# Middle rows of a folded Fourier transform: broadcast into both mirror slots and halved in the tables, in place of a zero fill followed by a second transfer

## The chip, the cores and the metric

The kernel runs on one core of one Trainium2 chip. The metric is the device time of one execution in microseconds (us). Each kernel has several executions; the detailed trace of one of them was kept, and that one is called the profiled execution.

## The reference

The input x is 8 batches of 3008 rows of 256 numbers. It is Fourier transformed along the rows and then along the columns, and the real part is fed to a feed-forward block with a squared ReLU.

```python
X = np.fft.fft(x, axis=1)          # x: (8, 3008, 256)
X = np.fft.fft(X, axis=2)
t = X.real.reshape(24064, 256)
h = np.maximum(t @ w_in, 0.0)      # w_in: (256, 2048)
return h * h @ w_out               # w_out: (2048, 256)
```

Inputs and output are float32.

## The kernel before

The row transform is folded by symmetry: rows n, S-n, M-n and M+n (S = 3008, M = 1504) are brought together, so that a quarter of the table is enough. The rows of a batch lie in one tile `x4` with four slots: slots 0 and 1 hold rows going up and are loaded directly by SyncE. Slots 2 and 3 hold their mirror images and are fetched by GpSimd with an indirect gather in reversed order. Each of the first 126 partitions holds six consecutive rows of a slot. Four middle rows (n = 0, 752, 1504 and 2256) have fewer partners than the others, and the kernel before puts a copy of them on an extra partition, 126. That partition is first filled with zeros, for batch 0 by a DMA from a zero tile, and the middle rows are then put over the zeros by two more DMAs, which must wait for the zero fill.

```python
x4 = xp.tile([P, 4, NQ, D], F32, name="x4")
zt = const.tile([2 * NQ, 2 * D], F32, name="zt")
nc.vector.memset(zt, 0.0)
...
xm = x4[NP : NP + 1].rearrange("p s q d -> p (s q) d")

def load_mid(b, eng):
    eng.dma_start(out=xm[:, 1 : NQ + 2 : NQ], in_=x[b : b + 1, 0 : M + 1 : M])
    eng.dma_start(out=xm[:, 3 : 3 * NQ + 3 : 3 * NQ - 1], in_=x[b : b + 1, QN : S : M])
...
nc.scalar.dma_start(out=x4[NP : NP + 1]..., in_=zt)      # zero fill of partition 126
for s in range(2):
    gather(0, 1 - s)                                     # GpSimd: slot 3, then slot 2
    nc.sync.dma_start(out=x4[0:NP, s, :, :], in_=up(0, s))   # SyncE: slot 0, then slot 1
```

The head of the program then runs: VectorE and ScalarE build sine and cosine tables in two halves (`red`, `trig`), GpSimd builds the column matrix and then issues the weights, TensorE runs dummy matmuls on the zeroed tile `ez` ahead of the real work, meant to bring its clock up (in this kernel's trace they start 0.43 us apart at first and 0.21 us apart from 16.07 us on, and the full clock is on record from 16.03 us), and VectorE folds batch 0 (`u`, then `v`, then `w`).

```python
pv.memset(csD[:, 0, 0, P - 1 : P], 1.0)                  # GpSimd
pv.memset(ez, 0.0)
...
for c in range(4):                                       # GpSimd's queue
    nc.gpsimd.dma_start(out=wst[:, :, cs], in_=moe_w_in[:, cs]...)
nc.gpsimd.dma_start(out=wot, in_=moe_w_out...)
for h in range(2):
    for f in rd0[5 * h : 5 * h + 5] + (tr0[3:] if h else tr0[:3]):
        f()
    if h == 0:
        load_mid(0, nc.scalar)
        alt_vecs()
dmats_fin()
sgn_vecs()
for f in mi0 + fe[0:3] + rd1[0:2]:                       # fe: the folds of batch 0
    f()
dmats_hi()
for _ in range(18):
    mm(warm, ez[:, 0, 0, :], ez[:, 0, 0:4, :], True, True)
for f in fe[3:]:
    f()
gcast(0, nc.scalar.copy)                                 # waits for the first weights
gmat(0)
for _ in range(4):
    mm(warm, ez[:, 1, 0, :], ez[:, 1, 0:4, :], True, True)
```

The first fold pair reads slots 0 and 3, and the second reads slots 1 and 2. Both read all 127 partitions, so both need the middle rows. After the fold come the matmuls of the row transform (`pf`), and from then on the main stream (`xb`, `po`).

Of the kernel before, what the change touches and what calls it, by code (L numbers as in the profile page):

```python
# [9 lines left out]
F32 = mybir.dt.float32  # L10
F16 = mybir.dt.float16
I32 = mybir.dt.int32
AF = mybir.ActivationFunctionType
ALU = mybir.AluOpType
# [8 lines left out]
def kernel(  # L23
# [7 lines left out]
    nc = tc.nc  # L31
    B, S, D = x.shape
    _, F = moe_w_in.shape
    P = 128
    M = S // 2
    QN = M // 2
    NQ = 6
    NP = QN // NQ + 1
# [14 lines left out]
    const = ctx.enter_context(tc.tile_pool(name="const", bufs=1))  # L53
# [15 lines left out]
    ts = nc.vector.tensor_scalar  # L69
    stt = nc.vector.scalar_tensor_tensor  # L70
    act = nc.scalar.activation

    def mm(o, l, r, start, stop):
        nc.tensor.matmul(o, l, r, start=start, stop=stop, skip_group_check=True)  # L74

    def iota(name, shape, pattern, base, mult, dt=F32):
        t = const.tile(shape, dt, name=name)
        nc.gpsimd.iota(t, pattern=pattern, base=base, channel_multiplier=mult,
                       allow_small_or_imprecise_dtypes=True)
        return t  # L80

    idx = iota("idx", [P, 1], [[0, 1]], NP - 1, -1, I32)
    pidx = iota("pidx", [P, 1], [[0, 1]], 0, 1)
    nvec = iota("nvec", [P, NQ], [[1, NQ]], 1, NQ)
# [3 lines left out]
                   allow_small_or_imprecise_dtypes=True)  # L88

    x4 = xp.tile([P, 4, NQ, D], F32, name="x4")  # L90
    zt = const.tile([2 * NQ, 2 * D], F32, name="zt")
    ez = const.tile([P, 2, NQ, P], F16, name="ez")
    nc.vector.memset(zt, 0.0)

    def up(b, s):
        return bass.AP(tensor=x.tensor, offset=x.offset + (b * S + s * M + 1) * D,
# [15 lines left out]
    xm = x4[NP : NP + 1].rearrange("p s q d -> p (s q) d")  # L112

    def load_mid(b, eng):
        eng.dma_start(out=xm[:, 1 : NQ + 2 : NQ], in_=x[b : b + 1, 0 : M + 1 : M])
        eng.dma_start(out=xm[:, 3 : 3 * NQ + 3 : 3 * NQ - 1], in_=x[b : b + 1, QN : S : M])

    def load_x(b):
        for s in range(2):
# [1 line left out]
            gather(b, 1 - s)  # L121
        load_mid(b, nc.gpsimd)

    nc.scalar.dma_start(out=x4[NP : NP + 1].rearrange("p s q d -> p (s q d)")
                      .rearrange("p (a c) -> p a c", a=2 * NQ), in_=zt)
    for s in range(2):
        gather(0, 1 - s)
        nc.sync.dma_start(out=x4[0:NP, s, :, :], in_=up(0, s))
# [6 lines left out]
    wS = 2.0 * math.pi / S  # L135
    wD = 2.0 * math.pi / D

    def vec(name, w=1):
        return const.tile([P, w], F32, name=name)

    top = vec("top")
    ts(out=top, in0=pidx, scalar1=float(NP), scalar2=None, op0=ALU.is_equal)
    nval = vec("nval", NQ)
    stt(out=nval, in0=nvec, scalar=QN - 0.5, in1=nvec, op0=ALU.is_lt, op1=ALU.mult)
    stt(out=nval[:, 3:4], in0=top, scalar=float(QN), in1=nval[:, 3:4], op0=ALU.mult, op1=ALU.add)
    hpi = vec("hpi")
    nc.vector.memset(hpi, math.pi / 2)
    hpl = vec("hpl")
    ts(out=hpl, in0=pidx, scalar1=NP - 1.0, scalar2=math.pi / 2, op0=ALU.not_equal, op1=ALU.mult)
    sgn = vec("sgn")  # L150
    s3 = vec("s3")
    nsgn = vec("nsgn")
# [16 lines left out]
    def sgn_vecs():  # L169
        ts(out=sgn, in0=pidx, scalar1=P - 1.5, scalar2=None, op0=ALU.is_lt)  # L170
        ts(out=s3, in0=sgn, scalar1=-2.0, scalar2=None, op0=ALU.mult)
        ts(out=sgn, in0=sgn, scalar1=2.0, scalar2=-1.0, op0=ALU.mult, op1=ALU.add)
        ts(out=nsgn, in0=sgn, scalar1=-1.0, scalar2=None, op0=ALU.mult)

    def absval(o, i):
        ts(out=o.bitcast(I32), in0=i.bitcast(I32), scalar1=0x7FFFFFFF, scalar2=None,
           op0=ALU.bitwise_and)
# [5 lines left out]
    def dmats():  # L183
        pv = nc.gpsimd
        t = tgp.tile([P, P], F32, name="td", tag="td")
        m = tgp.tile([P, P], F32, name="md", tag="md")
        pv.tensor_scalar(out=m, in0=jrow, scalar1=pidx[:, 0:1], scalar2=None, op0=ALU.mult)
        pv.tensor_scalar(out=t, in0=m, scalar1=1.0 / D, scalar2=R23, op0=ALU.mult, op1=ALU.add)
        pv.tensor_scalar(out=t, in0=t, scalar1=R23, scalar2=-float(D),
                         op0=ALU.subtract, op1=ALU.mult)  # L190
        pv.tensor_tensor(m, m, t, op=ALU.add)
        pv.memset(csD[:, 0, 0, P - 1 : P], 1.0)
        pv.memset(ez, 0.0)  # L193

        def fin():
            absval(t, m)
            nc.vector.tensor_copy(csD[:, 0, 1, P - 1 : P], alt)
            act(csD[:, 0, 1, 0 : P - 1], m[:, 0 : P - 1], AF.Sin, bias=0.0, scale=wD)
            act(csD[:, 0, 0, 0 : P - 1], t[:, 0 : P - 1], AF.Sin, bias=hpi[:, 0:1], scale=-wD)

        def hi():
            ts(out=csD[:, 1, :, 0:P:2], in0=csD[:, 0, :, 0:P:2], scalar1=-1.0, scalar2=None,
               op0=ALU.mult)
            nc.vector.tensor_copy(csD[:, 1, :, 1:P:2], csD[:, 0, :, 1:P:2])
        return fin, hi

    cosT = const.tile([P, NQ, HE + HO], F16, name="cosT")
    sinT = const.tile([P, NQ, HE + HO], F16, name="sinT")
    BLK = ((0, HE), (HE, HO))

    def table_ops(blk):
        c0, n = BLK[blk]
        ng = (n + 1) // 2
        nm = n // 2
        cs = slice(c0, c0 + ng)
        tb = {}
        hq = NQ // 2
        kb = krow[:, blk : blk + 1, 0:ng].to_broadcast([P, hq, ng])

        def red(h):  # L220
            qs = slice(h * hq, (h + 1) * hq)

            def views():
                return tb["t"][:, qs, 0:ng], tb["m"][:, qs, 0:ng]

            def nk():
                if h == 0:
                    tb["t"] = tgp.tile([P, NQ, HG], F32, name="tt", tag=f"tt{blk}")
                    tb["m"] = tgp.tile([P, NQ, HG], F32, name="tm", tag=f"tm{blk}")
                vt(views()[1], nval[:, qs].unsqueeze(2).to_broadcast([P, hq, ng]), kb, op=ALU.mult)  # L230

            def near():
                t, m = views()
                ts(out=t, in0=m, scalar1=1.0 / S, scalar2=R23, op0=ALU.mult, op1=ALU.add)

            def turns():
                t, m = views()
                ts(out=t, in0=t, scalar1=R23, scalar2=-float(S), op0=ALU.subtract, op1=ALU.mult)  # L238

            def rest():  # L240
                t, m = views()
                vt(m, m, t, op=ALU.add)  # L242

            def size():
                t, m = views()
                absval(t, m)

            return [nk, near, turns, rest, size]

        def trig(h):  # L250
            qs = slice(h * hq, (h + 1) * hq)

            def cos(qs, bias):
                return lambda: act(cosT[:, qs, cs], tb["t"][:, qs, 0:ng], AF.Sin,
                                   bias=bias[:, 0:1], scale=-wS)

            r = [lambda: act(sinT[:, qs, cs], tb["m"][:, qs, 0:ng], AF.Sin, bias=0.0, scale=wS)]
            if h == 0:
                return r + [cos(slice(0, 1), hpi), cos(slice(1, hq), hpl)]
            return r + [cos(qs, hpl)]  # L260

        src = slice(c0, c0 + nm)
        dst = slice(c0 + n - 1, c0 + n - 1 - nm, -1)

        def mir(d, a, qs, sv):
            o, i = d[:, qs, dst], (d if qs.start % 2 else a)[:, qs, src]
            if blk == 0:
                return lambda: act(o, i, AF.Copy, bias=0.0, scale=sv[:, 0:1])
            return lambda: ts(out=o, in0=i, scalar1=sv[:, 0:1], scalar2=None, op0=ALU.mult)

        qg = (slice(0, 5, 4), slice(2, 3), slice(1, 6, 4), slice(3, 4))
        return (red(0) + red(1), trig(0) + trig(1),
                [mir(cosT, sinT, qs, sv) for qs, sv in zip(qg, (nalt, alt, alt1, nalt))]
                + [mir(sinT, cosT, qs, sv) for qs, sv in zip(qg, (nalt, alt, nalt1, alt))])
# [167 lines left out]
    for g in range(0, NPAIR, CH):  # L442
# [3 lines left out]
        while o < n:  # L446
            b, i = divmod(g + o, NK)
# [90 lines left out]
    rd0, tr0, mi0 = table_ops(0)  # L538
    rd1, tr1, mi1 = table_ops(1)
    dmats_fin, dmats_hi = dmats()  # L540
    for c in range(4):
        cs = slice(c * F // 4, (c + 1) * F // 4)
        nc.gpsimd.dma_start(out=wst[:, :, cs],
                          in_=moe_w_in[:, cs].rearrange("(c p) f -> p c f", p=P))
    nc.gpsimd.dma_start(out=wot, in_=moe_w_out.rearrange("(c p) o -> p c o", p=P))
    for h in range(2):
        for f in rd0[5 * h : 5 * h + 5] + (tr0[3:] if h else tr0[:3]):
            f()
        if h == 0:
            load_mid(0, nc.scalar)  # L550
            alt_vecs()
    dmats_fin()
    sgn_vecs()
    for f in mi0 + fe[0:3] + rd1[0:2]:
        f()
    dmats_hi()
    warm = psx.tile([P, 512], F32, name="warm", tag="x")

    for _ in range(18):
        mm(warm, ez[:, 0, 0, :], ez[:, 0, 0:4, :], True, True)  # L560
    for f in fe[3:]:
        f()
    gcast(0, nc.scalar.copy)
    gmat(0)
    for _ in range(4):
        mm(warm, ez[:, 1, 0, :], ez[:, 1, 0:4, :], True, True)
    gcast(1, nc.scalar.copy)
    gcast(2, nc.vector.tensor_copy)
# [13 lines left out]
    def spread(ops, lo, hi):  # L582
        for i, f in enumerate(ops):
            side.setdefault(lo + int((hi - lo) * i / len(ops)), []).append(f)
# [8 lines left out]
    spread([(lambda c=c: wcast(c)) for c in range(4)], 3, 7)  # L593
    spread(rd1[2:], 1, 8)
    spread(fo, 7, 12)
    spread(tr1[0:3], 6, 8)
    spread(tr1[3:], 8, 9)
    spread(mi1, 9, 12)
    spread(stage1_ops(0, 1, True), 11, 15)
    FOLD = {0: [(1, 0.35, 0.52)], 1: [(2, 0.02, 0.2), (3, 0.38, 0.56), (4, 0.7, 0.85)],  # L600
# [37 lines left out]
    for f in mmq:  # L638
        p = f()
# [32 lines left out]
```

## Time and profile before

| | before |
|---|---|
| time, median of 3 | 659.51 us (659.0 to 660.09) |
| span of the profiled execution (its time was 661.0 us) | 659.22 us |
| landings of x: slots 0, 1, 3, 2 | 6.24, 9.45, 12.15, 14.67 us |
| last middle row landed | 14.66 us |
| first weights: issued, landed | 10.04, 15.75 us |
| first fold pair starts | 14.59 us |
| first `pf` matmul | 21.54 us |
| 19th `pf` matmul (start of the second block) | 45.01 us |
| span minus that | 614.21 us |

The landings and the last rows of this table are read from the trace's DMA and matmul records, counted from the start of the span. At 661.0 us the profiled execution is 1.5 us above the median of the three others, so this trace shows a slower execution than usual.

Two lines of the page's part on the chain that ended last show what bounds the program (share of the span by engine, then by line):

```profile
PE 93%; DVE 4%; DMA 2%; ACT 1%; issue 0%; DVEq 0%
PE po L74 50%; PE xb L74 37%; PE pf L74 6%; DMA x<-zt 1%; DMA x<-in_x_dram 1%; DVE u L314 1%; DVE h L534 0%; DVE h L532 0%; DVE wout L591 0%; DVE v L322 0%; DVE tm L242 0%; DVE tm L230 0%; ACT r L520 0%; DVE w L327 0%; DVE tt L238 0%
```

TensorE (PE) carries 93% of the chain. The change does not touch that stream, so only the other 7%, which lies almost entirely at the start, can move.

The chain in the first 25 us of the kernel before (start in us, length in us, what):

```profile
0.91 0.48 DVE zt L93
1.43 6.74 DMA x<-zt
...
8.19 6.28 DMA x<-in_x_dram
...
14.59 1.82 DVE u L314 x2
...
21.54 3.08 PE pf L74 x18
```

The zero tile, its transfer and the transfer of the middle rows stand one behind the other and end at 14.46 us. The fold follows at once.

The timeline of the same kernel, three instructions of VectorE and two of GpSimd (start, length, engine, line, operation, tiles, and in brackets the engine's idle time just before and what ended it):

```profile
8.46 1.94 DVE L176 TENSOR_SCALAR tt<-tm 128x567 int32<-128x567 int32 x1
14.59 1.82 DVE L314 TENSOR_TENSOR u<-x 127x765 f16<-127x765 f32 x2 [3.38 <-DMA x<-in_x_dram]
21.14 1.16 DVE L327 TENSOR_TENSOR w<-v 127x381 f16<-127x381 f16 x4
```

```profile
8.71 1.37 POOL L193 MEMSET ez<- 128x1536 f16 x1
10.04 3.08 POOL L543 DMA_DIRECT2D wst<-in_moe_w_in_dram  x4
```

VectorE idles for 3.38 us until the middle rows are there. VectorE's absolute-value step took 1.94 us beside GpSimd's memset, where the same step of the first half took 0.46 us.

The view of waits for the first 47 us names the same wait, and a small one for the weights (engine, line, what ended the waiting: us in total, times, longest):

```profile
DVE u L314 <- DMA x<-in_x_dram: 3.4, 1, 3.4
ACT win L282 <- DMA wst<-in_moe_w_in_dram: 0.7, 1, 0.7
```

### The profile page before, as it was taken

What the parts mean: (1) busy time and instruction counts of PE and PEld (TensorE: products, weight loads), DVE (VectorE), ACT (ScalarE), POOL (GpSimd) and SP (SyncE); (2) the same over time, 40 slices, a digit from 0 to 9 for tenths busy, and PEclk for the clock granted to TensorE, in tenths of its full rate; (3) what the DMA queues carried; (4) which work ended last, traced back from release to release, by engine and by line L of the source; (5) the groups of instructions that cost most, each with busy time, mean ns of one, the idle gap of its engine ahead of it and who ended that gap; (6) DMA issues with size and microseconds to landing.
All of it is one profiled execution on the core that took longest, in us unless ns stands there. A gap on an engine that the chain in (4) does not pass through costs nothing.

```text
span 659.2 us, 14938 instructions
## 1 busy us (share of the span) xinstructions
PE 637.7 (97%) x5958; PEld 550.5 (84%) x5958; DVE 404.0 (61%) x1076; ACT 519.0 (79%) x930; POOL 52.2 (8%) x67
## 2 busy tenths in 40 slices
PE   3779999999999999999999999999999999999998
PEld 1358889888798889888898887988899888998886
DVE  7899559679677554865558555455555555444451
ACT  5687777887788888888888887888888888888883
POOL 7203003123020000400000000000000000000000
PEclk9999999999999999999999999999999999999999
DMA  8927217286354111721111101011111111111111
GB/s 265 304 66 186 81 36 213 73 221 157 99 140 133 47 38 44 194 77 49 33 49 33 50 33 49 33 45 39 46 35 49 34 49 41 41 45 45 42 49 50
DMA packets 33756, 54.65 MB, mean 83 GB/s; under 512 B 4438, under 2 KB 28534, under 8 KB 33686
## 3 DMA queue, kind: packets, MB, share of 16 engines
q0 software_dynamic: 6256, 27.45, 15.4%
q1 hardware_dynamic: 27398, 26.22, 12.5%
q8 instruction: 46, 0.75, 0.5%
q14 instruction: 24, 0.20, 0.1%
q10 hardware_dynamic: 32, 0.03, 0.0%
HBM read 29.00 MB, written 24.64 MB: 81 GB/s over the span
## 4 chain that ended last, share of the span: by engine, by line
PE 93%; DVE 4%; DMA 2%; ACT 1%; issue 0%; DVEq 0%
PE po L74 50%; PE xb L74 37%; PE pf L74 6%; DMA x<-zt 1%; DMA x<-in_x_dram 1%; DVE u L314 1%; DVE h L534 0%; DVE h L532 0%; DVE wout L591 0%; DVE v L322 0%; DVE tm L242 0%; DVE tm L230 0%; ACT r L520 0%; DVE w L327 0%; DVE tt L238 0%
## 5 line engine op out<-in xcount | busy, mean ns | idle before, releaser
L74 PE MATMUL po<-wout,h 128*128 128x256 f16 (+1 forms) x3040 | 452.7, 272 | 0.0
L74 PE MATMUL xb<-qt,G 128*128 128x256 f16 (+8 forms) x1760 | 332.2, 257 | 3.3 <-ACT r L520 2.6
L74 PEld LDWEIGHTS <-h 128*128 128x128 f16 (+1 forms) x3040 | 289.9, 97 | 33.6 <-issue 0.2
L534 DVE TENSOR_TENSOR h<-r 128x512 f16<-128x512 f16 (+1 forms) x384 | 160.5, 418 | 239.8 <-ACT r L530 239.1
L520 ACT ACTIVATE r<-xb 128x512 f16<-128x512 f32 (+1 forms) x384 | 226.4, 590 | 98.0 <-PE xb L74 85.8
L74 PEld LDWEIGHTS <-G 128*128 128x128 f16 x2640 | 237.7, 97 | 44.9 <-issue 10.2
L530 ACT ACTIVATE r<-xb 128x512 f16<-128x512 f32 (+1 forms) x384 | 226.2, 589 | 20.4 <-PE xb L74 2.3
L74 PE MATMUL xb<-pt,G 128*128 128x256 f16 (+8 forms) x880 | 187.8, 257 | 0.7 <-ACT G L292 0.3
L532 DVE TENSOR_TENSOR h<-r 128x512 f16<-128x512 f16 (+1 forms) x384 | 158.1, 412 | 0.0
L464 ACT ACTIVATE os<-po 128x512 f32<-128x512 f32 (+1 forms) x95 | 56.3, 592 | 4.0 <-PE po L74 4.0
L74 PE MATMUL pf<-cosT,w 127*128 127x377 f16 (+1 forms) x96 | 28.9, 325 | 2.2 <-DVE w L327 1.8
L314 DVE TENSOR_TENSOR u<-x 127x765 f16<-127x765 f32 x32 | 29.0, 947 | 3.4 <-DMA x<-in_x_dram 3.4
L74 PE MATMUL pf<-sinT,w 127*127 127x377 f16 (+1 forms) x96 | 28.9, 325 | 0.0
L104 POOL DMA_INDIRECT x<-in_x_dram,idx x18 | 26.5, 1471 | 5.4 <-issue 5.1
L74 PEld LDWEIGHTS <-w 127*128 127x128 f16 (+1 forms) x192 | 22.4, 118 | 5.1 <-DVE w L327 2.3
L120 POOL DMA_DIRECT2D x<-in_x_dram x14 | 7.9, 561 | 217.0 <-DVE u L318 217.0
L327 DVE TENSOR_TENSOR w<-v 127x381 f16<-127x381 f16 x64 | 20.4, 352 | 0.0
L369 ACT ACTIVATE as<-pf 128x377 f32<-128x377 f32 (+5 forms) x32 | 15.5, 486 | 3.3 <-PE pf L74 3.0
L74 PEld LDWEIGHTS <-ez 127*128 127x128 f16 (+1 forms) x46 | 5.1, 113 | 15.4 <-POOL ez L193 10.1
L74 PE MATMUL warm<-ez 128*128 128x512 f16 x22 | 8.0, 537 | 10.1 <-POOL ez L193 10.1
L322 DVE TENSOR_TENSOR v<-u 127x768 f16<-127x768 f16 x32 | 16.7, 548 | 0.0
L405 DVE TENSOR_TENSOR pt<-pf,as 128x377 f16<-128x377 f32 (+1 forms) x16 | 8.8, 547 | 0.3
(92 smaller groups left out, 123.6 us busy)
## 6 DMA issues: line engine op xcount, KB each, us to landing
out_dram<-os SPq DMA_DIRECT2D x157, 128.0 KB
x<-in_x_dram POOLq DMA_DIRECT2D x14, 756.0 KB, 10.1
wst<-in_moe_w_in_dram POOLq DMA_DIRECT2D x4, 512.0 KB, 5.7
wot<-in_moe_w_out_dram POOLq DMA_DIRECT2D x1, 2048.0 KB, 13.8
x<-in_x_dram SPq DMA_DIRECT2D x2, 756.0 KB
x<-in_x_dram,idx POOLq DMA_INDIRECT x18, 11.1
x<-in_x_dram POOLq DMA_DIRECT2D x14, 2.0 KB, 10.5
out_dram<-os SPq DMA_DIRECT2D x2, 108.0 KB
```

Source lines behind the costliest of these rows:

```text
L74: nc.tensor.matmul(o, l, r, start=start, stop=stop, skip_group_check=True)
L104: nc.gpsimd.indirect_dma_start(out=x4[0:NP, 2 + s, q : q + rows, :].rearrange("p q d -> p (q d)"), out_offset=None, in_=bass.AP(tensor=x.t ...
L314: return lambda: vt(u[k, s, q0 : q0 + NQ // 2, 1:D], x4[k, s, q0 : q0 + NQ // 2, 1:D], x4[k, 3 - s, ::-1, :][:, q0 : q0 + NQ // 2, D - 1 : ...
L322: return lambda: vt(v[k, s, qs, :], u[k, 0, qs, :], u[k, 1, qs, :], op=ALU.subtract if s else ALU.add)
L327: return lambda: vt(w[k, i, q : q + 3, 0 : P - 1], v[k, s, q : q + 3, 1:P], v[k, s, q : q + 3, D - 1 : P : -1], op=ALU.add if i < 2 else A ...
L369: act(st["a"][0:m, :], st[0][0:m, :], AF.Copy, bias=0.0, scale=1.0) \
L405: vt(hi_, bp, a, op=ALU.subtract)
L464: act(os_[0:m], st["o"][0:m], AF.Copy, bias=0.0, scale=HS * HS)
L520: act(r[:, 0, :, 0:n], xb[:, :, 0:n], AF.Relu)
L530: act(r[:, 1, :, 0:n], xb[:, :, 0:n], AF.Relu)
L532: vt(h2[:, 0, :, 0:n], r[:, 0, :, 0:n], r[:, 0, :, 0:n], op=ALU.mult)
L534: vt(h2[:, 1, :, 0:n], rr, rr, op=ALU.mult)
```

## The change

Its intent is to make the middle rows independent of the zero fill. Rows 0 and 1504 are broadcast into all six places of partition 126 in both slots that mirror each other, so partition 126 is written whole and nothing in it has to be zeroed first. The fold then adds such a row to itself, and the table entry that it meets is halved to make up for that; the entries of the other five places are zero. Rows 752 and 2256 are used from where the ordinary loads put them, on partition 125, where they also meet themselves and are halved in the table. For batch 0 the rows are four transfers at the very start of ScalarE's queue. Besides that, the memset of `ez` moves from GpSimd to VectorE, the first half of each table takes five ScalarE activations in place of three, and four dummy matmuls fall away.

```diff
-    zt = const.tile([2 * NQ, 2 * D], F32, name="zt")
-    nc.vector.memset(zt, 0.0)
     def load_mid(b, eng):
-        eng.dma_start(out=xm[:, 1 : NQ + 2 : NQ], in_=x[b : b + 1, 0 : M + 1 : M])
-        eng.dma_start(out=xm[:, 3 : 3 * NQ + 3 : 3 * NQ - 1], in_=x[b : b + 1, QN : S : M])
+        for s in range(2):
+            row = x[b : b + 1, s * M : s * M + 1]
+            if b == 0:
+                for sl in (s, 3 - s):
+                    eng.dma_start(out=x4[NP : NP + 1, sl], in_=row.to_broadcast([1, NQ, D]))
+            else:
+                r = s * NQ + 1
+                r2 = (3 - s) * NQ + NQ - 2
+                eng.dma_start(out=xm[:, r : r2 + 1 : r2 - r], in_=row.to_broadcast([1, 2, D]))
-    nc.scalar.dma_start(out=x4[NP : NP + 1]..., in_=zt)
+    load_mid(0, nc.scalar)
...
-    stt(out=nval, in0=nvec, scalar=QN - 0.5, in1=nvec, op0=ALU.is_lt, op1=ALU.mult)
-    stt(out=nval[:, 3:4], in0=top, scalar=float(QN), in1=nval[:, 3:4], op0=ALU.mult, op1=ALU.add)
+    stt(out=nval, in0=nvec, scalar=QN + 0.5, in1=nvec, op0=ALU.is_lt, op1=ALU.mult)
+    hpe = vec("hpe")
+    ts(out=hpe, in0=pidx, scalar1=NP - 0.5, scalar2=math.pi / 2, op0=ALU.is_lt, op1=ALU.mult)
-    ts(out=hpl, in0=pidx, scalar1=NP - 1.0, scalar2=math.pi / 2, op0=ALU.not_equal, op1=ALU.mult)
+    ts(out=hpl, in0=pidx, scalar1=NP - 1.5, scalar2=math.pi / 2, op0=ALU.is_lt, op1=ALU.mult)
+    hph = vec("hph")
+    ts(out=hph, in0=hpl, scalar1=math.pi / 6, scalar2=None, op0=ALU.max)
+    wsh = vec("wsh")
+    ts(out=wsh, in0=hph, scalar1=4.0 / S, scalar2=None, op0=ALU.mult)
...
-        pv.memset(ez, 0.0)
...                                             # trig: the first half of the tables
-            r = [lambda: act(sinT[:, qs, cs], tb["m"]..., bias=0.0, scale=wS)]
-                return r + [cos(slice(0, 1), hpi), cos(slice(1, hq), hpl)]
+                return [sin(slice(0, hq, 2), wS), sin(slice(1, 2), wsh[:, 0:1]),
+                        cos(slice(0, 1), hpe), cos(slice(1, 2), hph), cos(slice(2, 3), hpl)]
...
         if h == 0:
-            load_mid(0, nc.scalar)
             alt_vecs()
     sgn_vecs()
+    nc.vector.memset(ez, 0.0)
-    for _ in range(18):
+    for _ in range(15):
         mm(warm, ez[:, 0, 0, :], ez[:, 0, 0:4, :], True, True)
-    for _ in range(4):
+    for _ in range(3):
         mm(warm, ez[:, 1, 0, :], ez[:, 1, 0:4, :], True, True)
-    spread(tr1[0:3], 6, 8)
-    spread(tr1[3:], 8, 9)
+    spread(tr1[0:5], 5, 8)
+    spread(tr1[5:], 8, 9)
```

More of the change, by code (lines that the diff above doesn't have):

```diff
@@ L122, in load_x @@
         load_mid(b, nc.gpsimd)
-    nc.scalar.dma_start(out=x4[NP : NP + 1].rearrange("p s q d -> p (s q d)")
-                      .rearrange("p (a c) -> p a c", a=2 * NQ), in_=zt)
+    load_mid(0, nc.scalar)
     for s in range(2):
@@ L255, in cos, with sin @@
                                    bias=bias[:, 0:1], scale=-wS)
-            r = [lambda: act(sinT[:, qs, cs], tb["m"][:, qs, 0:ng], AF.Sin, bias=0.0, scale=wS)]
+            def sin(qs, scale):
+                return lambda: act(sinT[:, qs, cs], tb["m"][:, qs, 0:ng], AF.Sin, bias=0.0,
+                                   scale=scale)
             if h == 0:
-                return r + [cos(slice(0, 1), hpi), cos(slice(1, hq), hpl)]
-            return r + [cos(qs, hpl)]
+                return [sin(slice(0, hq, 2), wS), sin(slice(1, 2), wsh[:, 0:1]),
+                        cos(slice(0, 1), hpe), cos(slice(1, 2), hph), cos(slice(2, 3), hpl)]
+            return [sin(qs, wS), cos(qs, hpl)]
         src = slice(c0, c0 + nm)
@@ L546 @@
     for h in range(2):
-        for f in rd0[5 * h : 5 * h + 5] + (tr0[3:] if h else tr0[:3]):
+        for f in rd0[5 * h : 5 * h + 5] + (tr0[5:] if h else tr0[:5]):
             f()
         if h == 0:
-            load_mid(0, nc.scalar)
             alt_vecs()
```

## The prediction

> **What bounds it now.** TensorE: busy 97% of 659.2 us, and 93% of the chain that ended last. From about 46 us on the chain is TensorE without a break. The change leaves that stage alone; only the head can move. The head's chain (timeline, chain of waits) is: zero-fill memset of zt, 0.48 us; zero-fill transfer, issued at 1.43, last landing 8.17; the two mid-row transfers, issued by ScalarE at 8.19 and 8.84, landing 14.46 and 14.66; first fold (u from x) at 14.59, after VectorE idled 3.4 us for it; two fold pairs with 1.6 us of table work between, v, w; first real matmul (pf) at 21.54. From there to 46 us VectorE is nearly saturated and on the chain, so a shift of its start passes through.
>
> **Removed.** The zero fill and the second transfer behind it. Mid rows are issued at about 1 us and should have landed by 9. Also GpSimd's memset of ez (8.71 to 10.08). In its shadow one VectorE table step (absolute value, 128x567) took 1.94 us against 0.46 for its twin. [...] VectorE's step ended 0.3 us after the memset.
>
> **Added.** VectorE: three tiny ops before the tables (about +0.2 us, since krow already held the first table step to 1.67), and the ez memset: estimate 0.75 us, from 0.48 us for zt's 512 words, here 768. ScalarE: two extra table activations in each half (estimate +0.3 us each, from 0.34 us spacing of 189-column ones), four issues at the start (about 0.6 us each, as the mid ones now), so its table load starts about 0.6 us later; but it is spared the issue that held it idle 3.75 us until 9.42. TensorE: four fewer warm-up matmuls, off the chain.
>
> **Next gate.** Landings in the trace, by transfer: x slot 0 at 6.24, slot 1 at 9.45, gathered slot 3 at 12.15, gathered slot 2 at 14.67. The first fold needs slots 0 and 3, so it cannot start before about 12.2. VectorE should be free by 10.8. So of 3.4 us of waiting some 2.3 are won, and about 1.3 us of wait stay, now on the gather. The second fold pair would come at about 15.7, after slot 2's 14.67. The first pf matmul moves to about 19.2. Warm-up should begin near 10.8 and end near 17, gmat follows, w is still last. The weight loads are issued 1.3 us earlier on the gathers' queue and may delay slot 3 by a few tenths. In 35 to 46 us the ScalarE halves cost up to 0.3 us, mostly hidden behind VectorE.
>
> **Sum.** 659.5 - 2.3 + 0.2 = 657.4 us, range 656.0 to 659.0: 0.3% faster, within 2%: 0.98; faster by over 2%: 0.01; slower by over 2%: 0.01.
>
> **What would show it.** First fold at 12.2 to 12.7, its wait ended by the gather, no zt in the chain; no 1.9 us absolute-value step; pf at about 19.2; from 46 us on the same intervals 2 us earlier; TensorE's busy time lower only by warm-up.
>
> **What would make it wrong.** (a) The gathers land later because weight traffic mixes in: less gain. (b) Gathers land earlier once GpSimd is free: more, at most to 10.8. (c) TensorE is still at its slow clock when gmat comes ([...] here the warm-up matmuls were spaced 0.43 us for 5.9 us, then 0.21): gmat and pf start later, up to 1 us lost. (d) The saturated stretch 21 to 46 us is held by weight arrivals or ScalarE instead, and absorbs part of the shift.

Two passages of it are cut, at the marks: each gave a reason that no trace of this study shows. The sum is 659.5 - 2.3 + 0.2 = 657.4 us.

## The result, and the profile after

Ratios here and below are the mean time of one kernel's fast runs over that of the other's fast runs of the same rounds, so they are not quite the ratio of the medians that stand beside them. In the later sessions the profiled execution is left out of them, from which all but one can be worked out again (for e1 it gives 0.9979, and all seven executions 0.9988, against the recorded 0.9976).

| | before | after |
|---|---|---|
| time, median | 659.55 us (4 runs of the same rounds) | 658.78 us (4 runs, 658.03 to 659.72) |
| ratio of means, 95% interval | | 0.9989 [0.9972, 1.0006] |
| span of the profiled execution | 659.22 us | 657.94 us |
| landings of x: slots 0, 1, 3, 2 | 6.24, 9.45, 12.15, 14.67 us | 6.54, 10.37, 13.23, 16.59 us |
| middle rows landed | 14.46, 14.66 us | 6.80 to 10.80 us |
| first weights: issued, landed | 10.04, 15.75 us | 8.85, 17.71 us |
| first fold pair | 14.59 us | 13.25 us |
| first `pf` | 21.54 us | 20.33 us |
| 19th `pf` | 45.01 us | 43.79 us |
| span minus that | 614.21 us | 614.15 us |

With four runs a side the interval just reaches 1. The same kernel measured again gave 0.9976 [0.9963, 0.999], so there is a gain, and it is small.

The two traces, of a 661.0 us execution before and a 659.72 us one after, say where it came from. The last row of the table is the whole program behind the second block of row transforms. It took 614.15 to 614.29 us in all 14 traces, whatever the kernel. All that differs between the kernels happens in the first 45 us. There the fold came 1.34 us earlier, the first `pf` 1.21 us, the 19th `pf` 1.22 us and the end 1.28 us: the shift at the fold passed through to the end with almost nothing lost.

The timeline after, the same three instructions of VectorE with the moved memset and the second fold pair in between:

```profile
8.58 0.63 DVE L185 TENSOR_SCALAR tt<-tm 128x567 int32<-128x567 int32 x1
10.14 0.70 DVE L565 MEMSET ez<- 128x768 uint32 x1
13.25 1.82 DVE L326 TENSOR_TENSOR u<-x 127x765 f16<-127x765 f32 x2 [2.42 <-DMA x<-in_x_dram,idx]
...
16.62 1.82 DVE L326 TENSOR_TENSOR u<-x 127x765 f16<-127x765 f32 x2
...
19.84 1.15 DVE L339 TENSOR_TENSOR w<-v 127x381 f16<-127x381 f16 x4
```

The 1.94 us step is gone and VectorE is free at 10.84. It still waits for 2.42 us, and what ended the wait is now the transfer `x<-in_x_dram,idx`: the gather of slot 3. The second pair has no wait of its own, but it started at 16.62, only 0.03 us after slot 2 had landed (16.59, before 14.67). So slot 2 is a gate of the same height: an earlier slot 3 alone would not have moved the second pair.

The view of waits after:

```profile
ACT win L294 <- DMA wst<-in_moe_w_in_dram: 3.9, 1, 3.9
...
PE pc L74 <- ACT win L294: 3.0, 1, 3.0
...
DVE u L326 <- DMA x<-in_x_dram,idx: 2.4, 1, 2.4
```

ScalarE's wait for the first weights grew from 0.7 to 3.9 us. The chain of waits after has accordingly left the middle rows and goes over the weights:

```profile
8.85 8.86 DMA wst<-in_moe_w_in_dram
17.71 0.02 issue
17.73 1.05 ACT win L294
...
20.50 2.90 PE pf L74 x18
```

These weights were issued 1.2 us earlier than before and landed 2.0 us later. Part of the page on DMA issues gives the median time from issue to landing (last column, us) of the two weight tensors. Before:

```profile
wst<-in_moe_w_in_dram POOLq DMA_DIRECT2D x4, 512.0 KB, 5.7
wot<-in_moe_w_out_dram POOLq DMA_DIRECT2D x1, 2048.0 KB, 13.8
```

After:

```profile
wst<-in_moe_w_in_dram POOLq DMA_DIRECT2D x4, 512.0 KB, 8.9
wot<-in_moe_w_out_dram POOLq DMA_DIRECT2D x1, 2048.0 KB, 18.8
```

That the chain names the weights and not the fold is a matter of a tenth of a microsecond. The weights' branch gave its last dummy matmul at 20.50, which held the first `pf` 0.49 us behind the start of the first `w` (19.84). Before, when `w` alone held it, the distance was 0.40 us (21.14 to 21.54). Fold and weights have become two gates of nearly the same height.

### The profile page after: what moved, and what is told of

It reads as the page before. It is cut to its first block, busy times and chain, and to the rows that moved or that the text cites. A ratio compares the mean times of both kernels' runs of the same rounds, so it can differ in the third digit from the quotient of the medians.

```text
span 657.9 us, 14937 instructions
## 1 busy us (share of the span) xinstructions
PE 635.4 (97%) x5954; PEld 550.0 (84%) x5954; DVE 403.3 (61%) x1078; ACT 519.3 (79%) x934; POOL 50.9 (8%) x66
## 4 chain that ended last, share of the span: by engine, by line
PE 94%; DVE 3%; DMA 1%; POOL 1%; ACT 1%; issue 0%; POOLq 0%; DVEq 0%
PE po L74 50%; PE xb L74 37%; PE pf L74 6%; DMA wst<-in_moe_w_in_dram 1%; POOL x L102 0%; DVE h L546 0%; DVE h L544 0%; DVE wout L603 0%; DVE tm L250 0%; ACT r L532 0%; ACT win L294 0%; PE ps L74 0%; DVE tt L246 0%; DVE v L334 0%; DVE tt L185 0%
## 5 line engine op out<-in xcount | busy, mean ns | idle before, releaser
L74 PEld LDWEIGHTS <-ez 127*128 127x128 f16 (+1 forms) x42 | 4.4, 107 | 14.7 <-DVE ez L565 10.9
L74 PE MATMUL warm<-ez 128*128 128x512 f16 x18 | 5.8, 484 | 10.9 <-DVE ez L565 10.9
## 6 DMA issues: line engine op xcount, KB each, us to landing
x<-in_x_dram POOLq DMA_DIRECT2D x14, 2.0 KB, 10.8
```

The costliest lines, as they stand in the source:

```text
L74: nc.tensor.matmul(o, l, r, start=start, stop=stop, skip_group_check=True)
```

## The experiments

Three questions were open.

1. Is it really the early start of the middle rows that pays, or one of the change's by-products (GpSimd freed of its memset, VectorE's 1.94 us step gone)?
2. Why did slot 3 land at 13.23 instead of 12.15, the 1.1 us by which the fold fell short of the prediction? One theory says that the weights, issued earlier on the gathers' queue, mix in with the gathers. A rival says that the four row transfers at the head of ScalarE's queue hold up the loads of x. A second rival says that it is scatter.
3. Does the clock of TensorE take some of the gain back?

The texts below name these theories in short. Twelve kernels ran in three sessions of four, each session on one chip. All gave correct results, and all verdicts are "the same" at 2% (h2 and h3, with one execution each, have none). Diffs are against the changed kernel.

| kernel | median us (n) | ratio to before, 95% | slot 3 | first weights: issued, landed | first fold | first `pf` | 19th `pf` |
|---|---|---|---|---|---|---|---|
| before (first trace) | 659.51 (3) | | 12.15 | 10.04, 15.75 | 14.59 | 21.54 | 45.01 |
| after (first trace) | 658.78 (4) | 0.9989 [0.9972, 1.0006] | 13.23 | 8.85, 17.71 | 13.25 | 20.33 | 43.79 |
| e1 after again | 659.04 (7) | 0.9976 [0.9963, 0.999] | 14.48 | 7.31, 19.23 | 14.50 | 23.02 | 47.01 |
| e2 weights held | 658.68 (6) | 0.9987 [0.9969, 1.0005] | 10.92 | 10.46, 15.75 | 10.99 | 18.39 | 41.86 |
| e3 rows on SyncE | 659.58 (6) | 0.9993 [0.9968, 1.0019] | 13.42 | 7.30, 17.74 | 13.45 | 20.40 | 43.87 |
| e4 memset on GpSimd | 659.33 (6) | 0.999 [0.9965, 1.0016] | 13.13 | 8.64, 17.21 | 13.15 | 20.98 | 45.2 |
| h1 other order of x | 660.32 (6) | 0.9992 [0.997, 1.0014] | 11.16 | 9.68, 18.94 | 11.37 | 22.62 | 46.71 |
| h4 order, early warm-up | 661.99 (6) | 1.0017 [0.9998, 1.0036] | 9.48 | 9.67, 17.58 | 10.66 | 21.54 | 45.35 |
| h2 before again | 660.45 (1) | | 11.58 | 10.32, 15.10 | 14.03 | 20.98 | 44.45 |
| h3 e2 again | 657.73 (1) | | 10.93 | 10.42, 15.62 | 10.95 | 18.34 | 41.81 |
| k1 held, early warm-up | 658.70 (6) | 0.9968 [0.9949, 0.9987] | 12.69 | 10.19, 16.58 | 12.71 | 19.67 | 43.13 |
| k2 18 warm-ups | 659.20 (6) | 0.9973 [0.9955, 0.999] | 13.58 | 7.30, 17.89 | 13.61 | 20.56 | 44.02 |
| k3 rows late | 660.27 (6) | 0.9999 [0.9979, 1.0019] | 12.39 | 7.30, 17.08 | 13.87 | 20.82 | 44.28 |
| k4 held, 18 warm-ups | 658.67 (6) | 0.9976 [0.9956, 0.9996] | 12.13 | 10.46, 15.89 | 12.15 | 19.10 | 42.56 |

The kernel before had in these sessions a median of 660.38 us (e), 660.65 (h) and 660.65 (k), from 11 runs each. The columns from slot 3 on are from the one profiled execution of each kernel, in us. That execution need not be a typical one: it was the slowest of its series for after, e1, h1 and k2, and the fastest for e2.

### The changed kernel again (e1)

No edit. It asks how far one trace of the same kernel differs from another.

> The changed kernel unaltered, to see how far the landings of its first transfers scatter from one execution to the next, and to narrow its ratio. Theory M (the missing 1.4 us went to the weight loads, which now stand 1.2 us earlier on the same queue and mix with the gathers): slot 3 of x lands again near 13.2 us and the first weight quarter near 17.7 us, within 0.4 us, first pf matmul near 20.4 us. Theory N (the profiled execution was an unlucky one, its 659.72 us being the slowest of four): slot 3 near 12.2, first weights near 15.8, pf near 19.3, and a median 1.5 to 2 us under the kernel before.

Neither theory's landings came. Slot 3 landed at 14.48 instead of 13.23, the first weights at 19.23 instead of 17.71, and the 19th `pf` came at 47.01 instead of 43.79. The median time (659.04 us) did not follow: the profiled execution was the slowest of the seven, at 662.95 us. So one trace of this kernel may lie 3 us from another, and a difference of about 1 us between two single traces proves little. This is why the landings are compared below over groups of traces.

Part of the 3.2 us is the late landing. The other part is TensorE's clock. In the view by windows, the column before the DMA share is the granted clock (PEclk), in e1:

```profile
18.90:22.20 3.30, 1.85 (x6) 0.68 (x6) 3.23 (x11) 1.86 (x3) 1.55 (x2) 0.77 1.02 364
20.70:24.00 3.30, 3.30 (x11) 1.25 (x9) 2.38 (x8) 2.13 (x3) 2.71 (x4) 0.50 1.02 351
```

The same windows in the first trace of the changed kernel:

```profile
18.90:22.20 3.30, 3.30 (x19) 1.88 (x19) 2.97 (x10) 2.41 (x4) 2.99 (x4) 1.00 1.03 361
20.70:24.00 3.30, 2.80 (x18) 1.85 (x17) 2.49 (x6) 1.74 (x3) 1.49 (x3) 1.00 1.03 351
```

In e1 TensorE ran at half speed (granted clock 0.50 from 20.7 to 24.0 us) just as the real matmuls began. The first `pf` started 1.66 us after the first `w`, instead of 0.49, and from the first `w` to the 19th `pf` it took 25.65 us (21.36 to 47.01) instead of 23.95 (19.84 to 43.79): 1.7 us lost.

### The weights held back (e2, its repeat h3, and k4)

The five weight transfers are issued behind a tiny GpSimd copy that reads a vector which VectorE writes only after the tables, as late as the kernel before issued them.

```diff
-    for c in range(4): nc.gpsimd.dma_start(out=wst[:, :, cs], ...)
-    nc.gpsimd.dma_start(out=wot, ...)
...
     sgn_vecs()
+    held = vec("held")
+    nc.gpsimd.tensor_copy(held, nsgn)
+    for c in range(4): nc.gpsimd.dma_start(out=wst[:, :, cs], ...)
+    nc.gpsimd.dma_start(out=wot, ...)
     nc.vector.memset(ez, 0.0)
```

> The changed kernel, but GpSimd first copies one small VectorE vector that is ready at about 10.0 us, so that the weight loads are issued at about 10.15 us as in the kernel before (10.04) instead of 8.85. Theory M: the gathers are free of weight packets for longer, slot 3 lands at 12.2 and slot 2 at 14.7, the first weights at about 15.8 although issued later, first pf matmul at about 19.3, and the kernel gains about 1 us over the changed one. Theory Q (the four row transfers on the ScalarE queue, 24 small packets, hold up the x loads): landings stay as in the changed kernel, first weights at 17.7 or later, no gain.

> The kernel with the weight loads held to about 10.2 us, unaltered, for a second trace. If holding the weights is what made slot 3 land at 10.92 us, it lands again under 11.5. If that execution was a lucky one (its x transfers were already ahead by 0.3 MB at 8 us, before any weight packet), slot 3 lands at 12 to 13.5.

> The kernel with held weights and 18 instead of 15 warm-ups. If mixing of weight packets with the gathers is what cost the changed kernel its gain, slot 3 lands near 10.9 us for the third time, first weights near 15.6, and the median is 0.5 to 1.5 us under the changed kernel of the same rounds (k2 stands for it). If the two early landings were chance, slot 3 lands at 12 to 14 us.

In these three traces slot 3 landed at 10.92, 10.93 and 12.13 us, earlier than in every trace with early weights (12.39 at the earliest); a fourth held kernel, k1 below, had 12.69. By the expectations h3 met the theory of mixing (under 11.5), while k4 fell into the range that was named there as the sign of chance (12 to 14). The weights, although issued later, landed earlier too: 15.75, 15.62 and 15.89 us. In e2 the fold did not wait at all (the timeline has no bracket); in k4 it waited 1.09 us for slot 3. The timeline's line of e2:

```profile
10.99 1.77 DVE L326 TENSOR_TENSOR u<-x 127x765 f16<-127x765 f32 x2
```

And of k4:

```profile
12.15 1.82 DVE L326 TENSOR_TENSOR u<-x 127x765 f16<-127x765 f32 x2 [1.09 <-DMA x<-in_x_dram,idx]
```

The spans of these executions were 656.0, 656.0 and 656.7 us, the three shortest of the 14 traces. But spans as short are on record for executions of the changed kernel whose traces were not kept: 656.2 us in its first series, 656.1 and 656.2 in e1.

The other executions do not show a gain. Leaving out each kernel's profiled execution, the ten executions of e2 and k4 had a mean of 659.36 us, and the fourteen of the changed kernel, e1 and k2 had 658.87 us. Holding the weights is thus a clear difference between the traces and no gain in the times. The traces alone cannot say why the two differ, and this stays open; that a profiled execution was often the slowest of its series, or for e2 the fastest, is a rival that no run excludes.

### The rows on SyncE's queue (e3)

The four row transfers are issued by SyncE behind its two loads of x, instead of by ScalarE ahead of them.

```diff
-    load_mid(0, nc.scalar)
     for s in range(2):
         gather(0, 1 - s)
         nc.sync.dma_start(out=x4[0:NP, s, :, :], in_=up(0, s))
+    load_mid(0, nc.sync)
```

> The changed kernel, but the four row transfers are issued by SyncE after its two x loads instead of by ScalarE before them. ScalarE's table load then starts at about 1 to 3 us instead of 4.16. Theory Q: x slots 0 and 1 land at 6.2 and 9.4 as before the change (6.54 and 10.37 in the changed kernel), slot 3 near 12.2, pf about 1 us earlier, 1 us faster than the changed kernel. Theory M: slot 3 and the first weights stay near 13.2 and 17.7, and the time is that of the changed kernel within 0.4 us.

The landings stayed where they were: slots 0, 1, 3 and 2 at 6.50, 10.96, 13.42 and 16.57 us (after: 6.54, 10.37, 13.23, 16.59). Nothing here supports the theory that the row transfers on ScalarE's queue delay the loads of x. One trace would prove little, but e2, h3 and k4 speak against it too: they keep the early rows on ScalarE's queue, and slot 3 landed at 10.92 to 12.13 us. The time of e3 (659.58 us) is no better than that of e1.

### The memset of ez back on GpSimd (e4)

```diff
         pv.memset(csD[:, 0, 0, P - 1 : P], 1.0)
+        pv.memset(ez, 0.0)
...
-    nc.vector.memset(ez, 0.0)
-    for _ in range(15):          # and range(3) for the second group
+    for _ in range(18):          # and range(4)
```

> The changed kernel with one part undone: ez is zeroed by GpSimd again, with the 18 and 4 warm-up matmuls of before. Weights are then issued at about 10.1 us again, VectorE's absolute-value step takes 1.9 us again, and VectorE is free at about 11.3 us, still ahead of the gather. Theory M: slot 3 lands at about 12.2, first fold there, first weights at about 15.8, pf at about 19.3: about 1 us faster than the changed kernel, that is the full 2 us gain over the kernel before. Theory Q or a cost of the changed tables: no faster than the changed kernel.

This was meant to undo one part and, by it, to delay the weights. It did not work out as an experiment: GpSimd's own chain happened to run faster, so the weights were issued at 8.64 us all the same (8.85 after). It shows one thing: with the memset back on GpSimd a step of VectorE is again stretched to 1.94 us, this time the step beside it, the rounding of the second half of the table. The two lines of e4's timeline, VectorE's and then GpSimd's:

```profile
7.06 1.94 DVE L243 TENSOR_SCALAR tt<-tm 128x567 f32<-128x567 f32 x1
```

```profile
7.32 1.37 POOL L202 MEMSET ez<- 128x1536 f16 x1
```

The stretched step is in both kernels one with a single input that overlaps the memset. It ended 0.3 us after the memset in both kernels (10.40 and 10.08 before, 9.00 and 8.69 here), and in both it had started 0.25 us ahead of it (8.46 and 8.71 us, 7.06 and 7.32). GpSimd's `tensor_scalar` from 6.90 to 7.78 us (before) did not do this: the step of VectorE beside it (at 7.18) took its usual 0.46 us. Which step is hit is not fixed: in h2, the second trace of the kernel before, with the memset at the same 8.71 us, the absolute-value step took only 0.59 us and the step behind it 1.48 (0.21 in the first trace):

```profile
8.46 0.59 DVE L176 TENSOR_SCALAR tt<-tm 128x567 int32<-128x567 int32 x1
8.97 1.48 DVE L176 TENSOR_SCALAR td<-md 128x128 int32<-128x128 int32 x1
```

The dummy matmuls of e4 began at 8.74, ended at 14.53 and left TensorE idle for 3.80 us, and its clock then fell as in e1 (0.53 in the window from 18.9 to 22.2 us). Three of its six executions had such a low clock.

### Another order of x (h1, h4)

If slot 3 gates the first fold, one may let it pass slot 1, which is needed later. In h1, slot 1 goes on GpSimd's queue between the gathers. h4 adds the rows on SyncE and `ez` zeroed by a ScalarE activation (sine with scale 0) at the very start, with 44 dummy matmuls from 3.56 us on.

```diff
-    for s in range(2):
-        gather(0, 1 - s)
-        nc.sync.dma_start(out=x4[0:NP, s, :, :], in_=up(0, s))
+    nc.sync.dma_start(out=x4[0:NP, 0, :, :], in_=up(0, 0))
+    gather(0, 1)
+    nc.gpsimd.dma_start(out=x4[0:NP, 1, :, :], in_=up(0, 1))
+    gather(0, 0)
```

> The changed kernel, but the load of x slot 1, which only the second fold pair needs, no longer goes out beside slot 0 on SyncE's queue: GpSimd issues it between its two gathers, so that slots 0 and 3 have the transfer engines first. If the landing of slot 3 gates the first fold (the theory that the gate moved from the mid rows to the gather), slot 3 lands near 8 to 9 us instead of 13.2, the first fold starts when VectorE is free at about 10.9, its wait for data is gone, and the second pair finds slots 1 and 2 landed by about 14.3. The first matmul is then held by the first weight quarter, near 19 to 19.5 us, so 1 to 1.5 us under the changed kernel. If the gate was elsewhere (weights or TensorE alone), the fold starts earlier but the time stays within 0.5 us of the changed kernel.

> The same order of x, and in addition: ez is zeroed by ScalarE with a sine of scale 0 right at the start, so VectorE saves 0.7 us; the row transfers are issued by SyncE behind slot 0; 44 warm-up matmuls start near 3.5 us. A candidate to beat both kernels: first fold near 10.2 us, second pair near 13.6, first pf matmul at 17.5 to 18.5, held by whichever of w and the first weights is later, and the time 2 to 3 us under the changed kernel. If the total of bytes through the transfer engines sets the head, the second pair waits for slot 2 until 14 or later and the gain shrinks to about 1 us.

The first fold no longer waits: it started at 11.37 (h1) and 10.66 us (h4). The second pair pays for it. Its lines in the timelines, h1:

```profile
17.92 1.82 DVE L327 TENSOR_TENSOR u<-x 127x765 f16<-127x765 f32 x2 [3.21 <-issue]
```

h4:

```profile
16.46 1.82 DVE L329 TENSOR_TENSOR u<-x 127x765 f16<-127x765 f32 x2 [1.89 <-issue]
```

The profile puts the wait down to "issue", but in h1 slot 2 landed at 17.84 us, and in h4 at 16.39, each 0.07 to 0.08 us before the fold. The order within x moves the wait from one pair to the other; in neither trace did all four slots and the weights together arrive clearly earlier. Slot 3 in h1 also missed its expectation (11.16 us instead of 8 to 9). h4 was meant as the version to beat both kernels and came out slowest of all (661.99 us). In its trace TensorE's clock fell back just before the real work, and the mean clock of all six executions (0.995 to 0.997) fits such a fall in each; that it is the whole cause was not tested. Its line in the view by windows:

```profile
18.90:22.20 3.30, 3.30 (x10) 1.24 (x9) 2.50 (x9) 2.13 (x3) 2.84 (x4) 0.50 1.03 369
```

Its dummy matmuls ended at 15.70 us and TensorE idled for 3.00 us before the first real matmul.

### The kernel before again (h2)

> The kernel before, unaltered, for a second trace. If landings scatter from execution to execution, the second mid row lands 1 us or more away from 14.46 us and the head (start of the first matmul after stage 1, 45.01 us in the first trace) moves with it, while the rest stays 614.2 us. If they do not scatter, all are within 0.3 us.

Slots 3 and 2 landed at 11.58 and 13.93 us and the middle rows at 13.91 and 14.12, so the first fold came at 14.03 (14.59 in the first trace). Here the chain over the zero fill gated the fold again, while slot 3 was there 2.5 us earlier. The landings moved by some 0.6 us, and the head with them (45.01 to 44.45), which lies between the two expectations.

### More dummy matmuls (k2), late rows (k3), held weights with early dummies (k1)

k2 only raises the dummy matmuls from 15 to 18. k3 changes only the time of the row transfers: they are issued where the kernel before issued its middle rows, behind the first half of the tables. k1 is e2 with `ez` zeroed by ScalarE and 24 dummy matmuls from 8.76 us on, without the second group.

```diff
# k2
-    for _ in range(15):
+    for _ in range(18):
# k3
-    load_mid(0, nc.scalar)
...
         if h == 0:
+            load_mid(0, nc.scalar)
             alt_vecs()
# k1: the diff of e2, and
         if h == 0:
+            act(ez.rearrange("p a q c -> p (a q c)"),
+                pidx[:, 0:1].to_broadcast([P, 2 * NQ * P]), AF.Sin, bias=0.0, scale=0.0)
             alt_vecs()
-    nc.vector.memset(ez, 0.0)
-    for _ in range(15):
+    for _ in range(24):
```

> The changed kernel with 18 warm-up matmuls in the first group again instead of 15. Theory C (15 cold warm-ups at 0.43 us last 6.4 us, sometimes too short to switch TensorE to its fast clock before the weight matmuls, which cost one of seven executions of the changed kernel about 3 us): no execution over 660.5 us and clock 1.0 in all; the median stays within 0.5 us of the changed kernel. If the slow clock comes from the idle time before the weight matmuls instead, executions with 0.997 still occur.

> The changed kernel with one part undone: the row transfers are issued again in the middle of ScalarE's table work (about 6 to 9 us) instead of first. Everything else, no zero fill included, stays changed. If the early row transfers are the part that paid, the last of the first pair's rows lands after slot 3 (13 us or later), the first fold waits for it, near 14 us, and the time returns to that of the kernel before within 0.5 us. If slot 3 and the weights are the gate anyway, the time stays that of the changed kernel.

> The kernel with the weight loads held to about 10.2 us, and in addition ez zeroed by ScalarE in its idle stretch near 7.4 us, 24 warm-up matmuls from about 9 us, and no second group of warm-ups. A candidate to beat both kernels: slot 3 at about 10.9 us as in the two traces with held weights, first fold there, first weights at about 15.6, first pf matmul at about 17.8, clock 1.0 in nearly every execution, 2 to 3 us (0.3 to 0.5%) under the kernel before and 1 to 1.5 us under the changed one. If the scatter of the transfers decides instead, no better than the changed kernel.

k2 met its expectation: no execution was over 660.5 us, and none had a slow piece of clock. k2 and k3 answer the first question. They ran on the same chip, against the same runs of the kernel before. With the rows early, k2 was at 0.9973 [0.9955, 0.999]; with the rows late, k3 was at 0.9999 [0.9979, 1.0019]. k3 has every other part of the change, but 15 dummy matmuls instead of 18. In k3's trace the rows landed at 12.12 to 15.24 us, and the fold waited for one of them and not for the gather. Its line in the timeline:

```profile
13.87 1.82 DVE L325 TENSOR_TENSOR u<-x 127x765 f16<-127x765 f32 x2 [2.31 <-DMA x<-in_x_dram]
```

So the gain hangs on the early rows; the other parts together gave nothing measurable. The two intervals overlap a little, so this is strong evidence and not proof, and in the two kept traces the 19th `pf` differs by only 0.26 us.

TensorE's clock is a rival here, since two of k3's six executions had a slow piece of clock (as explained below) and none of k2's. The record lets one set such executions aside, a choice made afterwards: then k3's mean is 660.08 us, k2's 659.20, and that of the kernel before, over the same rounds on the same chip, 660.64. In the same way all seven later kernels with early rows and the old order of x (e1 to e4, k1, k2, k4) lie 1.2 to 2.1 us under the kernel before of the same rounds, and k3 0.6 us. So the clock does not explain the difference.

k1 missed its landings (slot 3 at 12.69 us instead of 10.9, first `pf` at 19.67 instead of 17.8). Still it was the best ratio, 0.9968 [0.9949, 0.9987], some 2 us under the kernel before. It beats the kernel before; against the changed kernel it is not separable (k1 658.70, k4 658.67, k2 659.20 us on the same chip).

### The weights and the gathers, over all traces

Leaving out h1 and h4, which change the order of x, the traces fall into two groups by the time at which GpSimd issued the first weights.

| first weights issued | kernels | slot 3 landed, mean | first weights landed, mean |
|---|---|---|---|
| at 10.0 us or later | before, h2, e2, h3, k1, k4 | 11.73 us (10.92 to 12.69) | 15.78 us (15.10 to 16.58) |
| at 7.3 to 8.9 us | after, e1, e3, e4, k2, k3 | 13.37 us (12.39 to 14.48) | 17.81 us (17.08 to 19.23) |

In the group with the earlier issue the weights landed 2.0 us later, and slot 3 1.6 us later. No trace of one group lies in the other's range for the weights, and one pair overlaps for slot 3 (k1's 12.69 and k3's 12.39).

The view by windows shows what the DMA engines did meanwhile. The last two columns are the DMA share and GB/s. Before:

```profile
12.00:14.00 2.00, 2.00 (x7) 0.65 (x5) 0.00 (x0) 2.00 (x6) 2.00 (x3) 1.00 1.00 303
14.00:16.00 2.00, 2.00 (x6) 0.71 (x5) 1.41 (x2) 1.28 (x4) 0.28 (x1) 1.00 0.96 344
```

After:

```profile
12.00:14.00 2.00, 2.00 (x6) 0.75 (x5) 0.75 (x1) 1.86 (x5) 1.09 (x1) 1.00 1.04 284
14.00:16.00 2.00, 1.87 (x9) 0.69 (x8) 1.97 (x5) 0.00 (x0) 0.54 (x1) 1.00 0.99 267
```

With the weights held (k4):

```profile
12.00:14.00 2.00, 2.00 (x6) 0.71 (x5) 1.85 (x4) 2.00 (x6) 2.00 (x4) 1.00 0.99 316
14.00:16.00 2.00, 2.00 (x9) 0.82 (x8) 1.97 (x6) 0.26 (x2) 1.70 (x3) 1.00 0.90 322
```

In these windows the engines are as busy after the change and move less: 267 GB/s at a share of 0.99, against 344 at 0.96. This view alone doesn't separate the groups, as e2 too has 264 GB/s at 0.96 from 14 to 16 us. The packets do. A packet of x of 6144 bytes that started between 12 and 13 us took 238 ns (median) in the kernel before and 242 in k4, and 394 in the changed kernel, whose first weight packets started at 10.58 us. Over the groups it was 234 to 266 ns with late weights (only 2 and 4 packets in e2 and h3) and 390 to 428 with early ones. In the kernel before and in k4 they started at 12.10 and 12.47, when the gathers were nearly done (by 13 us, 244 and 231 of the 252 packets of the gathers had landed, against 204).

Two cautions stand. First, most of slot 3's delay is older than the weights: by 8 us, before any weight packet, the kernels with late weights had moved 1.76 to 2.05 MB, and those with early weights 1.70 to 1.82 MB. Slot 0 landed at 5.79 us in the mean of the first group and at 6.52 in the second, and slot 1 at 9.13 and 10.55. So 1.4 of slot 3's 1.6 us were there at slot 1. In three traces of the second group (after, e4 and k3) slot 1 landed before the first weight packet started (9.9 to 10.6 us); there it was 1.0 us later than in the first group, and slot 3 1.2. Until the weights are issued, e2 and h3 are the same program as the changed kernel and e1, and so are k4 and k2; what causes that part isn't settled. What the weights' packets can have added to slot 3 is then, by an estimate from these differences (1.6 less 1.4 us, 1.2 less 1.0), about 0.2 us; for slot 2 (14.10 and 16.68 us) and for the weights themselves there is more room. Second, as said, the other executions do not reward the hold.

### When the clock falls back

The records of the granted clock in the traces begin and end a whole number of pieces of 3.41 us apart. In e1 the full clock is on record from 17.25 to 20.67 us and the half one after it, until between 24.0 and 24.1 (in the view by windows the clock is 0.50 from 20.7 to 24.0 us and 1.00 from 24.1). In the first traces of the kernel before and of the changed kernel one record of the full clock lasts 645.12 us, 189 times 3.413, and begins at 16.03 us in the one and at 14.10 in the other. In e1, e4, h1 and h4 there is one slow piece (granted clock 0.50) at the start of real work, and the piece before it held little TensorE work: in e1 17.26 to 20.67 us, of which TensorE worked 0.86 us, in e4 15.70 to 19.11 with 0.78 us, in h1 17.07 to 20.48 with 1.0 us, in h4 15.43 to 18.84 with about 0.4 us. The idle time between dummies and real work was 2.55 us in e1, 3.80 in e4, 2.41 in h1 and 3.00 in h4. In the first trace of the changed kernel it was 2.96 us, longer than in e1 or h1, and the clock stayed up. There, if the pieces are counted on from the start of that record (14.10, 17.51, 20.93 us), which is the author's reading, as the record has no edge there, the pause of 15.87 to 18.83 fell across two pieces, each with over 1.7 us of work. In the kernel before, counted in the same way, the clock stayed up over a piece with 1.63 us (19.44 to 22.86).

On the way up, the full clock is on record from 14.10 us in the first trace of the changed kernel, after dummies from 10.89 on (0.43 us apart at first and 0.21 us apart from 14.19 on), and in e1 from 17.25 after dummies from 11.63 on. If pieces are counted back from that edge, again the author's reading, the full clock did not come after a piece with 2.2 us of dummies (10.43 to 13.84 in e1) or one with 2.48 us (9.20 to 12.62 in the kernel before), and came after one with 3.2 us (after) and one with 2.75 us (9.76 to 13.17 in h2). What decides about the clock was not tested on its own.

Executions with such a slow piece (taken from a mean granted clock below 0.9985) were 13 of 33 for the kernel before in the three sessions (mean 661.13 us, against 660.34 for the other 20), 1 of 11 for the changed kernel (662.95 against 658.86), 0 of 6 for k2 and k4, 1 of 6 for e2, e3 and k1, 2 of 6 for h1 and k3, 3 of 6 for e4 and 6 of 6 for h4. So the clock didn't take the change's gain back as a rule, though it can cost an execution some 2 us or more; those differences of whole executions contain late landings as well.

## Why the prediction was right

It was right in its range. The measured median of 658.78 us lies within 656.0 to 659.0, 1.4 us above the predicted 657.4. That it fell inside is partly luck: the same kernel had 659.04 us in e1, and k2 659.20, both just above the range, in sessions in which the kernel before was slower too.

- **What bounds the kernel and what can move.** Right. The rest behind the 19th `pf` took 614.21 us before and 614.15 after. The predicted "+0.2" for ScalarE's halved activations does not appear: from the first to the 19th `pf` it took 23.47 us before and 23.46 after.
- **The chain over the zero fill goes.** Right. The middle rows landed by 10.80 us (predicted by 9), the chain of waits has no zero tile, and k3, which issues the rows late again, loses the gain (0.9999).
- **The absolute-value step.** Right for the two traces: 1.94 us became 0.63. In h2 it took 0.59 us in the kernel before too, and the step behind it was stretched instead (1.48). e4 agrees that a step of VectorE is stretched beside GpSimd's memset: there it was another step that took 1.94 us. By what mechanism is not shown. VectorE was free at 10.84 us (predicted 10.8), and the memset of `ez` took 0.70 us (estimate 0.75).
- **The next gate.** Right in kind: the wait is now ended by the gather of slot 3. The size was off, and this is the term of the sum that was mis-sized. The prediction said that the weights "may delay slot 3 by a few tenths" and put the fold at 12.2 to 12.7. Slot 3 landed 1.08 us later than before in the first trace (13.23), so of the 2.3 us to be won at the fold 1.34 were won, and the first `pf` came at 20.33 instead of 19.2. In place of the 1.3 us of wait that were to stay, 2.42 us stayed. The second pair came at 16.62 instead of 15.7, just behind slot 2, whose landing the prediction had kept at 14.67 (16.59). Over the groups of traces the delay of slot 3 is 1.6 us. The prediction's cause of failure (a) had named weight traffic; that this was the cause is not shown. The traces of e2 and k4 put the first `pf` at 18.39 and 19.10 us, but in the first trace 0.92 of the 1.08 us were there at slot 1 (10.37 instead of 9.45), before the first weight packet at 10.58.
- **The weights as a second gate.** Missed. The prediction saw that they would be issued 1.3 us earlier and took it for granted that they would not land later. They landed 2.0 us later, and their branch gated the first `pf` in the trace, by some 0.1 us over the fold.
- **ScalarE's issues.** Mis-sized without effect: its table load started 1.35 us later (4.16 instead of 2.81), not 0.6. The timeline after shows the four issues as one group of 3.40 us, the first of 1.30 us and the others of 0.67 each. It was off the chain, as VectorE waited for x anyway.
- **The clock.** The possible loss (c), a clock that is still slow when `gmat` comes, happened in neither trace of the changed kernel. In e1 the clock had gone up at 17.25 us and fell back to 0.50 at 20.67, after a pause of 2.55 us, which the prediction had not foreseen; it cost 1.7 us.

What the times can and can't confirm: the predicted gain of 2.1 us would be a ratio of 0.9968. The three series of this kernel, k2 with three more dummies included, gave 0.9989, 0.9976 and 0.9973, which is 0.7, 1.6 and 1.8 us. The last two intervals hold the predicted ratio and the first just misses it. So the gain is some 0.7 to 1.8 us. How much of the missing rest is the weights' interference, in the executions whose traces were not kept, is open.

## What to carry to other kernels

When a wait on one transfer is removed, the next transfer becomes the gate, and its landing time in the old trace isn't its landing time in the new one (here slot 3 of x, at 12.15 us before and 13.23 after): ask what else is now issued earlier and will be in flight beside it (from 12 to 16 us the DMA share was 0.96 to 1.04 in the first traces of both kernels). In these traces, issuing a transfer that wasn't needed yet earlier went along with a later landing of both it (by 2.0 us in the means) and the urgent one (by 1.6); that it caused this is not shown, and the times do not confirm it. A pause between dummy matmuls and real work can cost: pauses of 2.41 to 3.80 us were followed by a granted clock of 0.50 in four traces (e1, e4, h1, h4), which cost 1.7 us in e1, while pauses of 2.40 us (e3) and 2.96 us (after) were not. Gains of 0.2% need repeated runs; single traces of one kernel here differed by 3 us. Look at earlier landings too before blaming a later transfer: here slot 1 was late before a weight packet had moved.
